# Batch 0's sequence transform folded like the other batches (sums in two equal parts, 60 products become 24), chunk 6 transposed by the DMA crossbar, and fewer, larger crossbar transposes for q and k

## The chip, the core and the metric

One NeuronCore of a Trainium2 chip runs the whole program. The metric is device time in microseconds (us) of one execution. The kernel before takes 269.62 us, the median of 5 runs (268.65 to 270.01). TensorE is called PE, VectorE DVE, ScalarE ACT, GpSimd POOL and SyncE SP, as the profile does. fp16 is used for all matrix operands.

## The reference

```
scores = scale * q @ k^T + bias            # 4 batches, 8 heads, 768 tokens, 64 per head
keep   = 8 global keys, or 0 <= rel < 96   # everything else is masked
x      = softmax(scores) @ v               # heads side by side: 4 x 768 x 512
mixed  = real(fft(fft(x, axis=1), axis=2))
u      = x + mixed
un     = (u - mean(u)) / sqrt(var(u) + 1e-6)
out    = u + relu(un @ w_ch1) @ w_ch2      # 512 -> 2048 -> 512
```

## The kernel before

**Stages of a batch.** Four batches run one after the other, overlapped as far as engines allow. A head pair `hp` (four of them in a batch) is the unit of attention, numbered n = 4b + hp.

1. `load` brings q, k and v of a head pair as fp32; `cast_qk` (batches 0 and 1) and `cast_direct` (batches 2 and 3) turn q and k into fp16.
2. `trans` turns q and k so that the head dimension lies on partitions. Batches 0 and 1 do it on PE with an evacuation (L527, L533, L537). Batches 2 and 3 use `trans_dma` (L506): four crossbar transposes of 64 partitions x 768 from the SP queue for each head pair, one for each half a of the partitions and each token parity t.
3. `score` (L564) makes three groups of banded scores for a head pair, ACT takes the exponential (L584, L587), DVE multiplies with the mask where batches are 2 or 3 (L599), `glob` (L643) adds the scores of the eight global keys, `av` (L691) multiplies with v, and DVE normalises (L710, L711) into X[b].
4. `bounce` writes X[b] to DRAM (L730) and reads it back in another row order as `xr` (L738).
5. The two FFTs are sums on DVE followed by products on PE. Batches 1 to 3 call `fold_s` (L755 to L774: sums that split the sequence of six blocks into residues of 6) and then `fold_d` (L849 to L866: the same along the model dimension, by residues of 4). Batch 0 calls `fold_3` instead (L808, L809, L820 to L830): it only adds and subtracts the two halves of the sequence, in parts of 256, 128 and 128 columns, so that `y_unit` (L892) needs three or six products for each of its 14 outputs, 60 in all, against 24 for another batch. These products use an extra table, `t1x` (480 KB, loaded at L1290 into a buffer of the ring `hT`).
6. `mirror` (POOL, L927 to L940) and `u_unit` (L972, L991 or L1000) end the second FFT, add `xr` and give u and un of a chunk. A batch has three chunks of 256 rows, c = 3b + pr. `nt_unit` turns un: chunks 0 to 6 on PE (L1063, eight matmuls and one evacuation at L1071 or L1073), chunks 7 to 11 by two crossbar transposes of 128 x 512 from SP (`nt_dma`, L1048).
7. `ph_unit` (L1091) multiplies with w_ch1, ACT or DVE evacuates with the relu (L1097, L1098), and `pg_unit` (L1114) or, for chunks 8 to 11, `pg_units` (L1195, seven products in place of eight) multiplies with w_ch2. DVE adds into u and SP stores.

**What sets the order.** The class `Plan` keeps a clock for each engine, costs written by hand, and landing times of some transfers (`LAND`), and issues work in the order in which it would start. So each engine has one fixed instruction list, and every engine and every DMA queue issues strictly in that list's order. PE works through four streams: MIX (y, u, turning of un), ATT, PH and PG. A change of a cost in `Plan` moves instructions but computes nothing else.

**Weights.** w_ch1 and w_ch2 come as eight DMAs that cast (POOL queue, L1345, L1350). They take over the buffers into which batch 1's q and k had been loaded, so the first is issued after the last cast of head pair 7. A small transfer (`hold`, L1359) reads the last piece of w_ch2; batch 2's loads wait for it through `("gate",)`.

**Buffers.** Rings of tiles: `qs` has 3 staging buffers for all loads of batches 2 and 3, `qk` 2 (fp16 q and k before turning), `hT` 3 (the hidden layer of a chunk, but also X[1]), `xx` 2 PSUM double banks plus C and D until the first `ph` takes their place.

Of the kernel before, what the change touches and what calls it, by code (L numbers as in the profile page):

```python
# [17 lines left out]
class Plan:  # L18
# [8 lines left out]
    LAND = {("xw", 0, 0): 36.0, ("xw", 0, 1): 37.6, ("xr", 0): 43.3, ("ld", 4, 2): 50.1, ("ld", 5, 2): 55.5, ("ld", 6, 2): 60.9,  # L27
            ("ld", 7, 2): 66.4, ("w1", 0): 45.8, ("w1", 1): 50.6, ("w1", 2): 54.3, ("w1", 3): 57.9, ("w2", 0): 61.6, ("w2", 1): 65.2, ("w2", 2): 68.1, ("w2", 3): 70.7}
    LAT = {"ACT": 0.14, "DVE": 0.12, "POOL": 0.08}

    def __init__(self):
        self.t = {"PE": 0.0, "ACT": 0.0, "DVE": 0.0, "POOL": 0.0, "SP": 0.7, "DMA": 1.9, "DMA2": 0.0}
        self.tok = {}
        self.ready = []
        self.pending = []
        self.rings = {}
        self.left = {}
        self.n = 0

# [23 lines left out]
    def later(self, ways, needs=(), after=0.0, outs=(), uses=(), ring=None, lat=0.0, dma=0.0, then=None, rank=1):  # L63

        self.n += 1
        self.pending.append((self.n, ways, list(needs), after, outs, uses, ring, lat, dma, then, rank))
        self.promote()
# [11 lines left out]
    def first(self):  # L79

        best = None
        for i, (ready, p) in enumerate(self.ready):
            c = (min(max(self.t[w[0]], r) for w, r in zip(p[1], ready)), p[10], ready[0], p[0], i)
            if best is None or c < best:
                best = c
        return best

    def emit(self, place):
        ready, (_, ways, needs, after, outs, uses, ring, lat, dma, then, _) = self.ready.pop(place)
# [5 lines left out]
        if dma:  # L95
            q = "DMA2" if eng == "ACT" or outs and outs[0][0] in ("xw", "xr") else "DMA"
# [5 lines left out]
        for u in uses:  # L102
            self.used(u, end + lat)
        if ring is not None:
            self.rings[ring].append(end + lat)
# [4 lines left out]
    def pe(self, us, after=0.0):  # L110
# [6 lines left out]
    LOOK = 10  # L117

# [60 lines left out]
def kernel(  # L179
# [24 lines left out]
    DB = 1  # L204
# [78 lines left out]
    NBUF = {"hT": 3, "qk": 2, "qs": 3, "qkT": 4, "er": 2, "eg": 1, "x": 1, "xr": 1, "zy": 1, "eA": 1,  # L283
# [43 lines left out]
    def load(b, hp, which):  # L327
# [3 lines left out]
        if b >= FB:  # L331
            srcs = [(0, q), (1, k)] if which == "qk" else [(2, v)]
            for w, src in srcs:
# [10 lines left out]
                pl.later([("SP", 0.55 if w < 2 else 1.1, run)], free("qs", i) + gate, 0.0, [("ld", n, w)], lat=1.7, dma=2.67)  # L344
# [55 lines left out]
    def cast_direct(b, hp, w, i):  # L400
        n = HP * b + hp

        def cast(on):
            if n not in qk16:
                qk16[n] = buf("qk", n, [P, 2, 2, NP, 2, Dh], FP16, 1)
            for t in range(2):
                copy_on(on, qk16[n][:, t, w], stage[("t", n, w)].rearrange("p (h i t) d -> p t i h d", h=2, t=2)[:, t])
        pl.later([("ACT", act(768), lambda: cast("ACT")), ("POOL", 1.6, lambda: cast("POOL"))],
# [7 lines left out]
    def cast_v0(b, hp):  # L416
        n = HP * b + hp

        def cast():
            V0[n] = buf("er", n, [P, NP, 2, 2, Dh], FP16, 1)  # L420
            nc.gpsimd.tensor_copy(V0[n].rearrange("p n t h d -> p (n t) h d"),
                                  stage[("t", n, 2)].rearrange("p (h n) (t d) -> p h (n t) d", h=2, t=2).rearrange("p h j d -> p j h d"))
        pl.later([("POOL", 0.87, cast)], [("ld", n, 2)] + free("er", n), 0.0, [("vc", n)], [("free",) + vat(n)], rank=b)

    def v_place(b, hp):
        n = HP * b + hp

        def run(start, ring):
# [14 lines left out]
            pl.used(("free", "er", n), e)  # L443
# [43 lines left out]

    def kg_copies(b, hp):
        n = HP * b + hp
        for s in range(2):  # L490
            def cp(s=s):
# [3 lines left out]
                    TT[n][64 * s:64 * s + 64, 1, 0:P].rearrange("p (t m) -> p t m", t=2)[:, :, 0:NG // 2])  # L495
# [3 lines left out]
    def trans_dma(b, hp):  # L499
        n = HP * b + hp  # L500

        def xb(a, t):
            if n not in TT:
                TT[n] = buf("qkT", n, [P, 2, S], FP16, 6)
            o = TT[n].rearrange("p w (i a t m) -> p a t (w i) m", a=2, t=2, m=64)[:, a, t]
            nc.sync.dma_start_transpose(o, qk16[n][64 * a:64 * a + 64, t].rearrange("p w i h d -> p (w i h d)"))  # L506
        at = [(a, t) for a in range(2) for t in range(2)]
        for x, (a, t) in enumerate(at):
            pl.later([("SP", 1.3, lambda a=a, t=t: xb(a, t))],
                     ([("qk", n, 0), ("qk", n, 1)] + free("qkT", n)) if x == 0 else [("xb", n, x - 1)], 0.0,  # L510
                     [("xb", n, x)], lat=0.0, dma=0.01)
        pl.later([("SP", 0.0, lambda: None)], [("xb", n, 3)], 0.0, [("qkT", n)], [("free", "qk", n)], lat=2.2, dma=0.5)
# [28 lines left out]

    def score(b, hp, g):
        n = HP * b + hp
        idx = 2 * HP + 3 * (n - 2 * HP) + g

        def run(start, ring):
            pa = bank(ring, f"sc_{n}_{g}")
            w0, w1_ = ((256, CO), (CO, CO), (256, P))[g]
            tiles = ((2 * g, 0, w0), (2 * g + 1, 256, w1_))
            if b < 2:  # L550
# [10 lines left out]
            for i, c0, cw in tiles:  # L561
                for s in range(2):
                    lo = 64 * s
                    nc.tensor.matmul(pa[:, s, c0:c0 + cw], TT[n][lo:lo + 64, 1, i * P:(i + 1) * P],  # L564
                                     TT[n][lo:lo + 64, 0, i * P:i * P + cw], start=(b > 1), stop=True,
                                     skip_group_check=(b < 2))
            e = pl.pe(0.24 if b > 1 else 0.66, start)
# [17 lines left out]
            if b < 2:  # L585
# [17 lines left out]
        ATT.append(([("qkT", n)] + ([("sid", hp), ("c", "dist")] if b < 2 else []), BANKS(b), run))  # L603
# [29 lines left out]
    def glob(b, halves):  # L633
# [4 lines left out]
        def run(start, ring):  # L638
            pg = bank(ring, f"pgl_{b}_{halves[0]}")
            for half in halves:  # L640
                for i in range(2):
                    hp = 2 * half + i
                    nc.tensor.matmul(pg[32 * half:32 * half + 32, 0, :], kG[b % 2][:, hp, :],  # L643
                                     TT[HP * b + hp][:, 0, 256:S], start=(i == 0), stop=(i == 1),
                                     tile_position=(0, 32 * half))
            e = pl.pe(mm_us(512, 2 * len(halves)), start)
# [14 lines left out]
    XT = [("x", 0), ("hT", 4), ("x", 1), ("x", 2)]  # L661
# [3 lines left out]
    def av(b, part, jp):  # L665
# [8 lines left out]
        def run(start, ring):  # L674
# [31 lines left out]
            def norm():  # L706
                if b not in X:
                    X[b] = buf(XT[b][0], XT[b][1], [P, NS, Dm], FP16, 4 if b else 5)
# [11 lines left out]
    def bounce(b):  # L720
# [3 lines left out]
        for n, (c0, c1) in enumerate(parts):  # L724
            def wr(n=n, c0=c0, c1=c1):
# [3 lines left out]
                for t in range(2):  # L729
# [3 lines left out]
                     lat=1.7, dma=2.4 if b else 2.6)  # L733
# [5 lines left out]
        pl.later([(on, 0.5, rd)], [("xw", b, n) for n in range(len(parts))] + free("xr", b), 0.0, [("xr", b)], lat=1.7, dma=3.8 if b else 2.4, then=None if b else (lambda t: pl.tok.__setitem__(("xi",), pl.t["SP"])))  # L739

    def fold_s(b):

        parts = ((0, 256), (256, 128), (384, 128)) if b == 0 else ((0, 512),)
        c = float(-np.sqrt(3.0) / 2.0)
        for n, (c0, cw) in enumerate(parts):
# [25 lines left out]
            def f4(c0=c0, cw=cw, cell=cell):  # L771
# [7 lines left out]
                     [("f1", b, n)], [("free",) + XT[b]] * (2 if len(hps) == HP else 1))  # L779
            pl.later([("DVE", 2 * dve2(2 * cw), f2)], [("f1", b, n)] + free("ww", IW(b, n)), 0.0, [("f2", b, n)])  # L780
            pl.later([("DVE", 4 * dve2(cw), f3)], [("f2", b, n)], 0.0, [("f3", b, n)])
            pl.later([("DVE", 2 * dve(cw), f4)], [("f3", b, n)], 0.0, [("z", b, n)],
                     [("free", "eA", IA(b, n)), ("free", "ww", IW(b, n))])
        return [("z", b, n) for n in range(len(parts))]

    def IA(b, n):

        return n if b < DB else 2 * b - DB + n

    def NA(b):  # L790
        return 0 if b < DB else 1

    def IW(b, n):

        return 2 * b + n if b < DB else 3 * b - DB + n
# [45 lines left out]
    def fold_d(b, needs):  # L841
# [30 lines left out]
        pl.later([("DVE", 0.95 + 1.0, g1)], needs + free("eA", ia) + free("ww", IW(b, NA(b))), 0.0, [("w", b, 0)])  # L872
        pl.later([("DVE", 0.95 + 1.15, g2)], [("w", b, 0)], 0.0, [("w", b, 1)], [("free", "zy", 2 * b)])
# [169 lines left out]
    def nt_dma(c):  # L1043
        for a in range(2):
            def xb(a=a):
                if a == 0:
                    UNT[c] = buf("unT", c, [P, ND, CH], FP16, 1)
                nc.sync.dma_start_transpose(UNT[c][:, :, a * P:(a + 1) * P], T[("un", c)][:, a])  # L1048
            pl.later([("SP", 1.3, xb)], [("un", c, a)] + (free("unT", c) if a == 0 else [("nx", c, 0)]), 0.0, [("nx", c, a)], lat=0.0, dma=0.01)
# [426 lines left out]
```

## Time and profile before

| | |
|---|---|
| median of 5 runs | 269.62 us |
| the profiled execution | 269.62 us, of which span 267.8 us, clock 0.999 |
| PE busy | 255.3 us, 95% |
| DVE busy | 172.0 us, 64% |
| ACT busy | 151.1 us, 56% |
| POOL busy | 61.4 us, 23% |
| DMA | 42.03 MB, mean 157 GB/s; software queue (weights) 9.3%, SP's queue 50.4% of 16 engines' span |
| crossbar transposes of q and k | 32, landing 3.6 us after issue (median) |
| crossbar transposes of un | 10, landing 2.4 us after issue (median) |
| weights | 8 DMAs of 512 KB, landing 19.0 us after issue (median) |

The profile is of one execution. The span is from its first to its last instruction; 1.8 us of the execution's time lie around it. A busy time counts every moment in which at least one instruction of the engine is under way. Matmuls are pipelined, so the time one takes up in a dense stretch is the distance between starts, not its own duration: 16 matmuls of 256 columns take 1.75 us in the chain of work, 0.109 us each, though each lasts 0.273 us. SPq and ACTq are the queues from which DMAs are issued; the time there is that of the issuing instruction.

### The profile page before, as it was taken

What the parts mean: (1) busy time and instruction counts of PE and PEld (TensorE: products, weight loads), DVE (VectorE), ACT (ScalarE), POOL (GpSimd) and SP (SyncE); (2) the same over time, 40 slices, a digit from 0 to 9 for tenths busy, and PEclk for the clock granted to TensorE, in tenths of its full rate; (3) what the DMA queues carried; (4) which work ended last, traced back from release to release, by engine and by line L of the source; (5) the groups of instructions that cost most, each with busy time, mean ns of one, the idle gap of its engine ahead of it and who ended that gap; (6) DMA issues with size and microseconds to landing.
All of it is one profiled execution on the core that took longest, in us unless ns stands there. A gap on an engine that the chain in (4) does not pass through costs nothing.

```text
span 267.8 us, 6248 instructions
## 1 busy us (share of the span) xinstructions
PE 255.3 (95%) x2540; PEld 181.4 (68%) x2540; DVE 172.0 (64%) x349; ACT 151.1 (56%) x263; POOL 61.4 (23%) x127
## 2 busy tenths in 40 slices
PE   8799899899999899999999999999999999999994
PEld 3454558477855776676575356759777668888883
DVE  4566863833399475861559967778998645525473
ACT  1479693987536737996591354896443345444300
POOL 1442398153010152322110316101100511010000
PEclk9999999999999999999999999999999999999999
DMA  7999959999579986996859895402072251311122
GB/s 212 290 292 305 326 178 224 216 216 212 137 134 257 274 162 136 225 190 146 217 108 204 191 304 138 99 2 42 0 174 103 59 100 39 81 40 42 39 82 78
DMA packets 75743, 42.03 MB, mean 157 GB/s; under 512 B 32834, under 2 KB 71746, under 8 KB 75714
## 3 DMA queue, kind: packets, MB, share of 16 engines
q1 hardware_dynamic: 68658, 32.71, 50.4%
q0 software_dynamic: 4224, 4.19, 9.3%
q10 hardware_dynamic: 2832, 4.72, 7.1%
q8 instruction: 20, 0.33, 0.5%
q14 instruction: 9, 0.07, 0.1%
HBM read 31.92 MB, written 9.44 MB: 154 GB/s over the span
## 4 chain that ended last, share of the span: by engine, by line
PE 64%; DMA 20%; DVE 5%; SPq 4%; POOL 2%; ACT 2%; issue 1%; ACTq 0%; POOLq 0%; DVEq 0%
PE ph L1091 25%; PE pg L1114 12%; DMA w<-in_moe_w_ch_dram 10%; PE pgD L1195 5%; DMA qs<-in_q_dram 5%; PE py L892 4%; PE pgA L1195 4%; PE sc L564 4%; DMA u<-in_v_dram 3%; PE pu L972 3%; PE pav L691 3%; DMA qs<-in_v_dram 2%; SPq L506 2%; PE sc L559 2%; SPq L372 1%
## 5 line engine op out<-in xcount | busy, mean ns | idle before, releaser
L1091 PE MATMUL ph<-unT,w 128*128 128x256 f16 x768 | 94.1, 273 | 2.7 <-ACT hT L1097 1.6
L1091 PEld LDWEIGHTS <-w 128*128 128x128 f16 x768 | 72.6, 98 | 17.1 <-issue 6.2
L1097 ACT ACTIVATE hT<-ph 128x512 f16<-128x512 f32 x78 | 46.2, 597 | 41.6 <-PE ph L1091 41.5
L1114 PE MATMUL pg<-w,hT 128*128 128x512 f16 x256 | 60.7, 379 | 0.0
L1114 PEld LDWEIGHTS <-hT 128*128 128x128 f16 x256 | 24.1, 98 | 23.4 <-issue 0.6
L587 ACT ACTIVATE ex<-sc 128x992 f16<-128x992 f32 (+2 forms) x24 | 20.9, 926 | 8.8 <-PE sc L564 8.8
L584 ACT ACTIVATE er<-sc 128x992 f16<-128x992 f32 (+2 forms) x24 | 21.7, 925 | 5.6 <-PE sc L564 5.1
L376 ACT ACTIVATE qk<-qs 128x384 f16<-128x384 f32 (+1 forms) x29 | 13.8, 528 | 13.4 <-DMA qs<-in_q_dram 5.1
L1098 DVE TENSOR_SCALAR hT<-ph 128x512 f16<-128x512 f32 x18 | 12.4, 691 | 11.2 <-PE ph L1091 11.2
L1123 DVE SCALAR_TENSOR_TENSOR u<-pg,sm,u 128x512 f32<-128x512 f32 x16 | 12.0, 748 | 11.2 <-PE pg L1114 11.2
L466 POOL CAST v<-qs 128x768 f16<-128x768 f32 x8 | 7.0, 880 | 51.7 <-DMA qs<-in_v_dram 51.7
L564 PE MATMUL sc<-qkT 64*128 64x256 f16 (+1 forms) x192 | 17.0, 262 | 0.9 <-ACT er L584 0.8
L599 DVE TENSOR_TENSOR ex<-er,mk 128x992 f16<-128x992 f16 (+2 forms) x24 | 15.1, 636 | 3.8 <-ACT er L584 3.7
L691 PE MATMUL pav<-v,ex 128*128 128x65 f16 x352 | 16.3, 193 | 1.0 <-DVE x L711 0.7
L691 PEld LDWEIGHTS <-ex 128*128 128x128 f16 x352 | 15.2, 97 | 2.4 <-DVE x L711 0.9
L564 PEld LDWEIGHTS <-qkT 64*128 64x128 f16 x192 | 5.9, 94 | 15.1 <-issue 13.3
L1038 POOL TENSOR_SCALAR sm<-sm 128x2 f32<-128x2 f32 x12 | 2.4, 202 | 58.1 <-ACT un L1031 58.0
L907 ACT ACTIVATE zy<-py 128x1024 f16<-128x1024 f32 (+1 forms) x12 | 10.1, 846 | 9.1 <-PE py L892 6.6
L940 POOL COPY ww<-zy 128x512 f16<-128x512 f16 x16 | 9.9, 651 | 22.7 <-PE py L892 20.5
L1031 ACT ACTIVATE un<-un 128x512 f16<-128x512 f16 x24 | 14.9, 626 | 0.1
L991 DVE SCALAR_TENSOR_TENSOR u<-pu,xr 128x512 f32<-128x512 f32 x18 | 11.7, 690 | 4.8 <-PE pu L972 3.2
L1195 PEld LDWEIGHTS <-hT 128*128 128x128 f16 x128 | 12.5, 98 | 1.6
(129 smaller groups left out, 381.9 us busy)
## 6 DMA issues: line engine op xcount, KB each, us to landing
out_dram<-u SPq DMA_DIRECT2D x24, 256.0 KB, 2.4
w<-in_moe_w_ch_dram POOLq DMA_DIRECT2D x8, 512.0 KB, 19.0
qs<-in_q_dram SPq DMA_DIRECT2D x9, 384.0 KB, 5.7
qs<-in_k_dram SPq DMA_DIRECT2D x9, 384.0 KB, 5.3
qs<-in_v_dram SPq DMA_DIRECT2D x16, 192.0 KB, 4.2
xr<-xd ACTq DMA_DIRECT2D x3, 768.0 KB, 5.5
u<-in_v_dram SPq DMA_DIRECT2D x5, 384.0 KB, 6.9
w<-in_q_dram SPq DMA_DIRECT2D x4, 384.0 KB, 6.6
```

What stands on the lines that cost most here:

```text
L376: A(d, s, AF.Copy)
L564: nc.tensor.matmul(pa[:, s, c0:c0 + cw], TT[n][lo:lo + 64, 1, i * P:(i + 1) * P], TT[n][lo:lo + 64, 0, i * P:i * P + cw], start=(b > 1), s ...
L584: A(mine(), cut(pa), AF.Exp, 0.0, 0.125)
L587: A(cut(expst[hp][:, :, g * 512:g * 512 + (384 if g == 2 else 512)]), cut(pa), AF.Exp, 0.0, 0.125)
L599: VT(o, mine(), m, op=ALU.mult)
L691: nc.tensor.matmul(po[:, jj, hh * 65:(hh + 1) * 65], lhsT, v16[b % 2][:, i, h, 0:65], start=(jp == 0 and a == 0), stop=(a == len(ops) - 1) ...
L1031: A(x, x, AF.Square, accum_out=MV[c][:, a, 2:3])
L1091: nc.tensor.matmul(ph[:, a * CH:(a + 1) * CH], W1[0][:, d, jb * P:(jb + 1) * P], UNT[c][:, d, :], start=(d == 0), stop=(d == ND - 1))
L1097: pl.later([("ACT", act(512), lambda: A(dst, ph, AF.Relu)), ("DVE", dve(512), lambda: V.tensor_scalar_max(dst, ph, 0.0))], [], e, [("h", c ...
L1098: ("DVE", dve(512), lambda: V.tensor_scalar_max(dst, ph, 0.0))],
L1114: nc.tensor.matmul(pg, HT[c][:, jb, t * P:(t + 1) * P], W2[0][:, jb, :], start=(jb == 0), stop=(jb == NJ - 1))
L1195: nc.tensor.matmul(o, lhs(j), rhs(j), start=(first and j == 0), stop=(j == NK - 1), skip_group_check=True)
```

## The change

- Batch 0 uses `fold_s` and `fold_d` like the others (`DB` is 0). Its sums run in two parts of 256 columns. `fold_3` and `y_unit`'s branch for it are no longer used, `t1x` isn't loaded, and the buffer indices of `hT`, `eA` and `ww` shift by one. These sums get rank -1 in the planner (`RF`), with a head start of 0.8 us (`AHEAD`).
- Chunk 6 is turned by the crossbar too, and a chunk's un takes one transpose of 128 x 1024 instead of two of 128 x 512. `unT` is laid out (a, d, m) instead of (d, a, m), and `ph_unit`'s moving operand has two runs of 128.
- q of batches 2 and 3 takes one crossbar transpose of 128 partitions x 768, k two of 64 partitions x 768, so three for a head pair instead of four. The cast of q or k becomes one instruction of 768 columns instead of two of 384. q's tokens then lie in another order, so `score` and `glob` read them with strides of 64 elements; a score tile that had 240 columns takes 256, and a `glob` product of 512 columns becomes two of 256.
- v of batches 0 and 1 gets a ring of its own (`v0`) instead of a share of `er`.
- The planner's figures change: landing times, packet times of DMAs, a model of eight DMA lanes, a cost of 0.1 us where PE changes to or from 64-row products. The instruction lists move with them.

The core of the diff (the planner's bookkeeping and index shifts are left out):

```diff
-    DB = 1
+    DB = 0
...
-    LAND = {("xw", 0, 0): 36.0, ("xw", 0, 1): 37.6, ("xr", 0): 43.3, ("ld", 4, 2): 50.1, ...
+    LAND = {("xw", 0, 0): 34.0, ("xw", 0, 1): 36.0, ("xr", 0): 41.0, ("ld", 4, 2): 47.7, ...
...
+            if p[11]:
+                ready = [max(r, self.lanes[p[11] - 1]) for r in ready]
+            c = (min(max(self.t[w[0]], r) for w, r in zip(p[1], ready)) - self.AHEAD * (p[10] < 0), p[10], ready[0], p[0], i)
...
-            for t in range(2):
-                copy_on(on, qk16[n][:, t, w], stage[("t", n, w)].rearrange("p (h i t) d -> p t i h d", h=2, t=2)[:, t])
+            copy_on(on, qk16[n][:, w].rearrange("p n t h d -> p (n t) h d"),
+                    stage[("t", n, w)].rearrange("p (h j) d -> p j h d", h=2))
...
+    def key_at(n, i):
+        return i * P if n < FB * HP else (i % 2) * 384 + (i // 2) * P
+
+    def tile_of(n, lo, w, i, nb=1):
+        x = TT[n][lo:lo + 64, w]
+        if n < FB * HP or w:
+            o = key_at(n, i)
+            return x[:, o:o + P].rearrange("p (t m) -> p t m", t=2)
+        if nb == 1:
+            return x.rearrange("p (i t a m) -> p i a t m", t=2, a=2, m=64)[:, i // 2, i % 2]
+        if i % 2 == 0:
+            return x.rearrange("p (i t a m) -> p i a t m", t=2, a=2, m=64)[:, i // 2]
+        o = (i // 2) * 256 + 64
+        return x[:, o:o + 384].rearrange("p (y q m) -> p y q m", y=2, m=64)[:, :, 0:3:2]
...
-            o = TT[n].rearrange("p w (i a t m) -> p a t (w i) m", a=2, t=2, m=64)[:, a, t]
-            nc.sync.dma_start_transpose(o, qk16[n][64 * a:64 * a + 64, t].rearrange("p w i h d -> p (w i h d)"))
+            if w == 0:
+                nc.sync.dma_start_transpose(TT[n][:, 0].rearrange("p (j x) -> p j x", x=P),
+                                            qk16[n][:, 0].rearrange("p n t h d -> p (n t h d)"))
+            else:
+                nc.sync.dma_start_transpose(TT[n][:, 1, 384 * a:384 * a + 384].rearrange("p (j x) -> p j x", x=64),
+                                            qk16[n][64 * a:64 * a + 64, 1].rearrange("p n t h d -> p (n t h d)"))
...
+                    if b >= FB:
+                        nb = 1 if cw == P else 2
+                        o = pa[:, s, c0:c0 + nb * P]
+                        o = o.rearrange("p (y t m) -> p y t m", y=2, t=2) if nb == 2 else o.rearrange("p (t m) -> p t m", t=2)
+                        nc.tensor.matmul(o, TT[n][lo:lo + 64, 1, key_at(n, i):key_at(n, i) + P], tile_of(n, lo, 0, i, nb), start=True, stop=True)
+                        continue
...
-        parts = ((0, 256), (256, 128), (384, 128)) if b == 0 else ((0, 512),)
+        parts = ((0, 256), (256, 256)) if b == 0 else ((0, 512),)
...
-        for a in range(2):
-            def xb(a=a):
-                if a == 0:
-                    UNT[c] = buf("unT", c, [P, ND, CH], FP16, 1)
-                nc.sync.dma_start_transpose(UNT[c][:, :, a * P:(a + 1) * P], T[("un", c)][:, a])
+        def xb():
+            UNT[c] = buf("unT", c, [P, 2, ND, P], FP16, 1)
+            nc.sync.dma_start_transpose(UNT[c].rearrange("p a d m -> p (a d) m"), T[("un", c)].rearrange("p a f -> p (a f)"))
...
-        if c >= 7:
+        if c >= 6:
             return nt_dma(c)
...
-        def t1x_load():
-            T1X[0] = buf("hT", 3, [P, 5, 384], FP16, 4 * DB)
-            nc.sync.dma_start(T1X[0].rearrange("p a b -> p (a b)"), t1x_d.ap())
```

## The prediction

> **What bounds the kernel now.** I read the busy shares first.
>
> ```profile
> PE 255.3 (95%) x2540; PEld 181.4 (68%) x2540; DVE 172.0 (64%) x349; ACT 151.1 (56%) x263; POOL 61.4 (23%) x127
> ```
>
> PE is the bound, but 95% doesn't say where the other time lies. So next the timeline of PE, for idle time with a releaser (start, duration, row, idle before).
>
> ```profile
> 53.94 2.91 PE L1091 MATMUL ph<-unT,w 128*128 128x256 f16 x24 [1.06 <-ACT ex L587]
> ...
> 88.18 1.03 PE L1091 MATMUL ph<-unT,w 128*128 128x256 f16 x8 [1.65 <-ACT hT L1097]
> ```
>
> These are the two largest stalls after the first microseconds. Setting matmul counts times distances between starts (0.109 us for 256 columns, 0.216 for 512, 0.056 for 128) against the clock, I find about 6 us lost from 5.8 to 37.5 us, none in the y products (37.46 to 44.02), 1.4 from there to 53.94, 1.9 from 82.9 to 89, about 1 in all from 104 to 170, and none from 170 to 253. From 170 on PE is solid: whatever is gained by then, or taken out of PE's work, reaches the end.
>
> Third, the chain of work, for what else holds the start of the middle.
>
> ```profile
> 37.53 3.54 PE py L892 x32
> ...
> 42.50 27.51 DMA w<-in_moe_w_ch_dram
> ```
>
> The weights land until 70.0 us and gate batch 2's loads (70.43). A PE that is ahead meets them.
>
> Fourth, DVE and SP, for the prices of what is added and removed (start, duration; the spacing of starts is what an instruction costs in a row).
>
> ```profile
> 35.39 1.58 DVE L829 TENSOR_TENSOR eA<-zy 128x1536 f16<-128x1536 f16 x1
> ...
> 80.33 0.68 DVE L761 TENSOR_TENSOR ww<-eA 128x1024 f16<-128x1024 f16 x1
> 80.92 0.68 DVE L762 TENSOR_TENSOR ww<-eA 128x1024 f16<-128x1024 f16 x1
> 81.53 0.41 DVE L766 TENSOR_TENSOR zy<-eA,ww 128x512 f16<-128x512 f16 x1
> 81.86 0.42 DVE L767 TENSOR_TENSOR zy<-eA,ww 128x512 f16<-128x512 f16 x1
> 82.20 0.28 DVE L768 TENSOR_SCALAR zy<-ww 128x512 f16<-128x512 f16 x1
> ...
> 83.26 0.68 DVE L773 SCALAR_TENSOR_TENSOR zy<-ww,eA 128x512 f16<-128x512 f16 x1
> ...
> 87.97 0.29 DVE L863 TENSOR_TENSOR ww<-eA 128x256 f16<-128x256 f16 x1
> ```
>
> ```profile
> 96.50 5.21 SPq L506 DMA_TRANSPOSE qkT<-qk  x4
> ...
> 169.24 1.20 SPq L1048 DMA_TRANSPOSE unT<-un  x1
> ...
> 212.10 2.50 SPq L1048 DMA_TRANSPOSE unT<-un  x2
> ```
>
> A crossbar transpose holds SP's queue for 1.2 to 1.3 us, whether it has 64 or 128 partitions.
>
> **What the Trainium skill says.** "TensorE: Matmul & The Clock Gate", section "Wait — 56ns, not 53.3ns?", gives a warm matmul N columns at 2.4 GHz plus about 2.5 ns: 109 ns for 256. The trace agrees (60 y products in 6.56 us). "VectorE: DVE Perf Modes", section on the TRN2 errata, says that an instruction pays a fixed latency, so many small ones pay it often. The trace agrees: 256 columns cost 0.20 us of spacing where 512 cost 0.335, so halving saves less than half. "DMA: Bandwidth & Descriptors", "Rules for kernel authors", advises one transfer of 128 partitions over two of disjoint halves. The rows above show this for SP's queue, not for transfer time, which no row before isolates.
>
> **PE's work.** Counted from the instruction lists of both programs. Batch 0's y: 60 products become 24, 36 x 0.109 = -3.93 us. Chunk 6: eight transposes leave, 8 x 0.056 = -0.45. Scores: 48 tiles of batches 2 and 3 get 16 columns more; the two heads of a pair run at once, so 24 x 16 / 2400 = +0.16. `glob`: 8 products of 512 become 16 of 256, +0.02. Strided reads of q and unT, taken at nothing: the turned q is already written, and the mask broadcast already read, in pieces at full rate; if a matmul of q cost 20% more, 0.3 x 24 groups x 0.2 = +1.4. Sum -4.2.
>
> **DVE's batch 0.** Old sums: 0.94 for the first part (24.31 to 25.25), 1.1 for the two others, then 3.9 (33.46 to 37.4). New, for each part of 256 columns: two of 768 (0.95), two of 512 (0.67), two of 256 (0.41), two scalings (0.3, half-size of a row of 0.20 spacing, bounds 0.2 to 0.4) and two combined ones (0.67; bounds 0.6 to 0.8): 3.0. Then 1.95, and 1.8 as at 86.99 to 88.8; it could be 2.4, since L829's 1.58 shows that this step slows when POOL works. Total 9.8 against 5.9. Where is it paid? The first part comes at 23.85 and pushes the normalisations behind it; DVE has 1.3 us of gaps there, and one evacuation of turned q and k goes to ACT, so x ends at about 32.0 instead of 31.5. Second part to 35.1, first group of sums 37.0, second 39 to 39.6. PE has the same scores and one more turning ahead of y, and gets there at 37.46 + 0.67 = 38.1. So the first y products don't wait, the later ones up to 1.5 us; four y tiles come in 2.6 us where they took 6.56, and their seven evacuations of 0.6 to 0.7 on ACT and DVE no longer hide: PSUM banks come free at about 40.2 to 41. I put the third unit of u at 47.6, and the first `ph` at 51.2 instead of 53.94, behind u's additions on DVE and the exponential of the global scores on ACT. That is 2.7 us, and one placing of v (0.3) is done already: 3.0 of the 3.93.
>
> **The weights' stage.** From 51.2 PE needs weight pieces. Issued 37 to 43, landing 19.0 us later in the median, the last at 70.0: one every 3.4 us or so. v of head pair 7 queues among them. The table without t1x: 480 KB at about 290 GB/s is 1.65 us that all behind it on SP may win; bound 0 if the weights' issue, after the last cast at 36 us, sets the pace. I take 1.2. The part of PE's list before the second half of batch 1's `av` (70.15 us) then ends at about 68.2 with one `pg` block (0.86) more done: 2.8 us ahead; without the 1.2, 1.6.
>
> **The stall at 88.** It came from the masks on ACT (1.35 us) ahead of an evacuation, after PE had run through ten `pg` blocks. In the new lists all masks come together behind the bounce, and PE has twelve `pg` blocks (10.4 us, to about 84.4) in front of chunk 2; y's sums are ready at about 85. So 1.65 comes back: 4.45 us ahead at 104.
>
> **Batches 2 and 3.** SP loses 8 transposes of q and k and 4 of un: 12 x 1.25 = 15 us of its queue (9 if a 128-row one costs 1.5 times). Before, head pair 10's casts waited until 102.9 for a `qk` buffer, freed by the last of these. Casts: 14 pairs of 0.94 us on ACT become 10 of 0.845, -4.7; POOL does 6 instead of 2, at 0.83, with v's casts, the mirror and the rstd behind them. PE stalls little there, so I book 0, from -1 to +1.
>
> **Chunk 6.** A wait is added: SP waits for un, then 1.2 to 2.5 us of issue and 2.4 us landing, in place of 0.45 + 1.02. Queued behind it on SP are k's last transposes and chunk 7. Cover, from the end of its u: in the old run 6.5 us passed until its `ph` (163.9 to 170.41), filled with `pg`, u and scores, and the new list has the same. Un is ready about 2.8 in, so 6.4 to 7.7 are needed: +0 to 1.2; I take 0.2.
>
> **Sum.** Ahead at 104 us by 4.45; chunk 6's PE work -0.45 and its wait +0.2; scores and `glob` +0.18; batches 2 and 3 otherwise 0: -4.52. The profiled execution took 269.62 us (span 267.8 and 1.8 around it), which is also the median: 269.62 - 4.52 = 265.1 us.
>
> **Rivals.**
> 1. *The weights take it back.* For it: 27.5 us of chain are their transfer, and PE arrives sooner. Against: chunks 0 and 1 hold 14 us of `ph` that need only w_ch1. If t1x frees nothing and two `pg` blocks wait for w_ch2, 1.6 us remain at 70 and the stall at 88 is half kept: -2.2, 267.4.
> 2. *The stalls vanish too.* Shorter SP and ACT queues and the end of both named stalls: -4.2 - 1.06 - 1.65 = -6.9, 262.7. Against it: evacuations of y are bunched.
> 3. *Slower, by chunk 6 on the crossbar.* If its transpose stands in SP's list behind head pair 15's load and transposes: 5.7 landing, 0.9 cast, three issues 3.9, its own 1.2 + 2.4 = 14.1 us against 6.5 of cover, 7.6 lost, 4.2 won: 273.0. It decides from a wait of 4.4 us. Against: these transposes were issued before 169 us in the old run, un of chunk 7 did not wait for them, and there are fewer.
> That the change doesn't do what it says is excluded by the instruction lists.
>
> **Chances.** Forecast (263.8 to 266.6) 0.45; rival 1 (to 268.6) 0.22; rival 2 0.20; rival 3 0.07; within 0.3%, about what a measurement of this kernel can tell from no change, 0.06. So faster 0.87, same 0.06, slower 0.07. Range 261.8 to 268.6: it leaves out the slower case, most of no change and the far end of rival 2.
>
> **What would show it.** Right: 24 y products in under 4.5 us; first `ph` near 51; no stall of over 1 us near 85; PE solid from about 166. Wrong: `ph` at 54 (DVE's sums cost more), idle PE between 56 and 68 with a DMA as releaser (rival 1), chunk 6's first `ph` waiting for unT (rival 3), or distances of more than 0.109 us in `ph`.

## The result, and the profile after

The changed kernel takes 271.72 us (median of 43 runs, 267.34 to 275.81), the kernel before 269.71 (median of 80 runs, 268.42 to 272.69). The ratio is 0.9991 with a 95% interval of 0.9972 to 1.001. It counts only runs within 1.5% of a kernel's fastest, which leaves out more than half of the changed kernel's, so it lies below the quotient of the medians, 1.0075. A gain isn't shown: by the ratio the two are the same, by the medians of all runs the changed kernel is 2.0 us slower, and its own runs spread over 8.5 us. The forecast, 265.1 us and faster with a chance of 0.87, did not come true; its range ended at 268.6.

The profiled execution took 270.91 us, span 268.8. First the busy shares.

```profile
PE 253.2 (94%) x2504; PEld 178.3 (66%) x2504; DVE 179.4 (67%) x367; ACT 146.7 (55%) x243; POOL 64.8 (24%) x129
```

PE has 2.1 us less to do than before and the span is 1.0 longer. So PE's work went and its waits grew. The timeline of PE shows which waits stand in place of the two shown of before:

```profile
40.68 1.03 PE L947 MATMUL py<-t,ww 128*128 128x256 f16 x8 [0.80 <-ACT qkT L571]
...
52.79 1.91 PE L1144 MATMUL ph<-unT,w 128*128 128x256 f16 x16 [1.17 <-DVE u L1055]
...
90.03 1.03 PE L1144 MATMUL ph<-unT,w 128*128 128x256 f16 x8 [1.59 <-ACT hT L1150]
...
101.46 0.27 PE L1027 MATMUL pu<-t,zy 128*128 128x128 f16 x2 [0.99 <-DVE u L1046]
```

The first `ph` comes 1.15 us sooner than before, and the stall at 88 has not gone: it stands at 90 with the same releaser, and others follow. Over 36 to 53 us PE is busy 14.47 of 17.00 where it was busy 16.88: in that stretch the work taken out of it became waiting.

ACT's timeline shows why its evacuation (L1150) comes so late.

```profile
77.61 5.13 ACT L1359 ACTIVATE mk<-dist 128x640 f16<-128x640 f16 x8 [2.50 <-issue]
88.65 0.84 ACT L392 ACTIVATE qk<-qs 128x768 f16<-128x768 f32 x1 [5.92 <-DMA qs<-in_k_dram]
88.73 0.36 ACTq L790 DMA_DIRECT2D xr<-xd  x1
89.40 0.58 ACT L1150 ACTIVATE hT<-ph 128x512 f16<-128x512 f32 x1
```

The masks are done at 82.7, as forecast. But the next instruction in ACT's list is the cast of k of head pair 9, and ACT stands idle for 5.92 us until that k has landed. Behind it wait the read of `xr` and the evacuation. The chain of work says why k came late (start, duration, what).

```profile
70.99 5.08 DMA qs<-in_v_dram
...
76.19 0.84 POOL v L482
...
77.04 5.86 DMA qs<-in_q_dram
...
82.96 1.23 POOL qk L396
...
84.20 0.38 SPq L388
```

Load, cast, load, cast, load, one after the other: q of pair 9 is issued the moment the cast of v of pair 8 ends, and k of pair 9 (84.20) the moment q's cast ends. The releasers in the trace, which are inferred, say that all three use the same one of the three `qs` buffers, and that the other two had been free since about 75 us; pair9_fixed and pair9_spoiled below confirm it. The same in SP's list:

```profile
77.04 0.37 SPq L388 DMA_DIRECT2D qs<-in_q_dram  x1
77.51 4.10 SPq L538 DMA_TRANSPOSE qkT<-qk  x1
84.20 0.38 SPq L388 DMA_DIRECT2D qs<-in_k_dram  x1
```

One transpose holds the queue for 4.10 us here. The prediction's 1.2 to 1.3 us isn't the whole range: in before, too, one at 80.47 held it for 2.71.

Last, DVE's sums for the second part of batch 0:

```profile
34.05 0.91 DVE L821 TENSOR_TENSOR zy<-eA,ww 128x256 f16<-128x256 f16 x1
34.89 0.90 DVE L822 TENSOR_TENSOR zy<-eA,ww 128x256 f16<-128x256 f16 x1
35.72 0.21 DVE L823 TENSOR_SCALAR zy<-ww 128x256 f16<-128x256 f16 x1
```

The first two take three times as long as the same sum in fold_in_turn (0.28, shown below); POOL casts two tiles of q and k at that time (33.92 to 35.66).

### The profile page after: what moved, and what is told of

Its sections match the earlier page's. It is cut to its first block, busy times and chain, and to the rows that moved or that the text cites. A ratio compares the mean times of both kernels' runs of the same rounds, so it can differ in the third digit from the quotient of the medians.

```text
span 268.8 us, 6141 instructions
## 1 busy us (share of the span) xinstructions
PE 253.2 (94%) x2504; PEld 178.3 (66%) x2504; DVE 179.4 (67%) x367; ACT 146.7 (55%) x243; POOL 64.8 (24%) x129
## 4 chain that ended last, share of the span: by engine, by line
PE 52%; DMA 25%; ACT 7%; DVE 6%; POOL 3%; issue 3%; SPq 3%; POOLq 0%; DVEq 0%; ACTq 0%
PE ph L1144 19%; PE pg L1167 13%; DMA w<-in_moe_w_ch_dram 9%; PE pgD L1248 5%; DMA out_dram<-u 5%; PE pgA L1248 4%; DMA qs<-in_v_dram 4%; DMA u<-in_v_dram 3%; DMA qs<-in_k_dram 3%; PE pav L743 2%; ACT er L629 2%; PE py L947 2%; DMA qs<-in_q_dram 2%; SPq L388 2%; PE pu L1027 2%
## 5 line engine op out<-in xcount | busy, mean ns | idle before, releaser
L1150 ACT ACTIVATE hT<-ph 128x512 f16<-128x512 f32 x75 | 44.6, 598 | 47.9 <-PE ph L1144 47.7
L1151 DVE TENSOR_SCALAR hT<-ph 128x512 f16<-128x512 f32 x21 | 14.5, 690 | 13.7 <-PE ph L1144 13.4
L644 DVE TENSOR_TENSOR ex<-er,mk 128x992 f16<-128x992 f16 (+2 forms) x24 | 17.5, 738 | 2.0 <-ACT er L629 1.6
L392 ACT ACTIVATE qk<-qs 128x768 f16<-128x768 f32 x11 | 9.3, 842 | 14.2 <-DMA qs<-in_k_dram 8.0
L763 DVE TENSOR_TENSOR x<-pav,rc 128x512 f16<-128x512 f32 (+1 forms) x21 | 12.9, 615 | 0.7
L1077 ACT ACTIVATE un<-u,sm 128x512 f16<-128x512 f32 x10 | 7.1, 721 | 11.4 <-DVE sm L1050 11.4
L962 ACT ACTIVATE zy<-py 128x1024 f16<-128x1024 f32 (+1 forms) x10 | 8.8, 899 | 7.0 <-PE py L947 6.4
```

The source lines that it names most:

```text
L644: VT(o, mine(), m, op=ALU.mult)
L763: VT(X[b][:, 2 * jp:2 * jp + 2, first * Dh:(first + nh) * Dh].rearrange("p j (h d) -> p j h d", d=Dh), pv[:, :, :, 0:Dh], rc.to_broadcast( ...
L1150: pl.later([("ACT", act(512), lambda: A(dst, ph, AF.Relu)), ("DVE", dve(512), lambda: V.tensor_scalar_max(dst, ph, 0.0))], [], e, [("h", c ...
L1151: ("DVE", dve(512), lambda: V.tensor_scalar_max(dst, ph, 0.0))],
```

## Experiments

"Before" and "after" are the two kernels. Times are medians in us, then their range, then the ratio to before with its 95% interval. Differences between kernels are differences of medians.

### The parts alone

**fold_alone**: before with only batch 0's sums folded.

```diff
-    DB = 1
+    DB = 0
...
-        parts = ((0, 256), (256, 128), (384, 128)) if b == 0 else ((0, 512),)
+        parts = ((0, 256), (256, 256)) if b == 0 else ((0, 512),)
...
```

> The kernel before with one part of the change: batch 0's sums in two parts of 256 columns as for the other batches, 24 products of y, no t1x table; transposes, chunk 6 and the planner's figures as before. Theory A (the 3.9 us of PE work are gained at first, and given back later by loads and transposes of batches 2 and 3): some 1 to 2.5 us faster than before, 267 to 268.6, and the first ph 1 to 3 us earlier than 53.94. Theory B (the longer sums on VectorE and the bunched evacuations eat the saving on the spot): within 0.5 us of 269.7, the first ph at 53 to 54.

Measured: 272.86 (270.88 to 274.48), 1.0105 [1.0067, 1.0142]: slower. First `ph` at 53.44, only 0.5 sooner, and one stall of 3.32 us at 110 (`ph` behind ACT's evacuation). The fold alone does not pay. Whether a stall this large, 57 us later, is the fold's own doing isn't settled by this run; fold_in_turn below tests it.

**undo_chunk6**: after with chunk 6 turned on PE again.

```diff
-        if c >= 6:
+        if c >= 7:
```

> The changed kernel with chunk 6 turned on PE again (eight matmuls and an evacuation), all else as changed. If the wait for the crossbar costs at chunk 6 what its PE work saved (0.45 us), the time stays within 0.5 us of the changed kernel; if it is what takes the gain back (stalls of 1.6 us between 160 and 180 us), it is 1.5 us or more faster.

Measured: 272.57 (268.28 to 275.34), 1.0027 [1.0, 1.0054]: 0.9 above after's median, with the same wide spread. Chunk 6 by the crossbar is not the loss.

**undo_qk**: after with the four transposes, the halved casts and the score tiles of 240 columns of before, under the new planner. The lines show one of its places.

```diff
...
-        for x, (w, a) in enumerate(((0, 0), (1, 0), (1, 1))):
+        for x, (a, t) in enumerate(at):
...
```

> The changed kernel with q and k of batches 2 and 3 turned as before: four crossbar transposes of 64 partitions for a head pair, casts in two halves, score tiles of 240 columns. Theory C (the crossbar transpose of 128 partitions is the slow part, it lands 5.1 us after issue in the median where one of 64 partitions took 3.6): 2 to 3 us faster than the changed kernel, about 267, and a narrower spread of times. Theory A: no gain, 270 to 272, since SP gets eight transposes more.

Measured: 286.66 (283.38 to 289.35), 1.055 [1.051, 1.059]. Much slower, by a list that falls apart in batch 3 (PE waits of up to 3.75 us between 160 and 182, and a granted clock down to about half there). This tells of a bad list, not of what a transpose costs.

### The staging buffers

The ring `qs` doesn't give its buffers out in turn: which one a load gets follows from the order in which the plan issues loads and casts. **slots_in_turn** is after with load i in buffer i mod 3; the lists of all engines stay as they are.

```diff
+        if tag == "qs":
+            return wk.tile(shape, dtype, tag=f"qs{i % 3}_", name=f"{tag}_{i}", bufs=1)
         return wk.tile(shape, dtype, tag=tag, name=f"{tag}_{i}", bufs=NBUF[tag])
```

> The changed kernel with the three staging buffers of batches 2 and 3 handed out strictly in turn; instruction lists and their order are the same. In the changed kernel k of head pair 9 is given the buffer that q of the same pair has just left (its load is issued at 84.20, when q's cast ends), while two buffers have been free since 75 us. Theory A: k of pair 9 is issued at about 81 or earlier, its cast on ScalarE no longer holds up the evacuation behind it, the stall at 90.03 (1.59 us) and the wait for xr until 100 shrink: 1.5 to 3 us faster than the changed kernel, 268 to 270. Theories B and C: within 0.5 us of it.

Measured: 267.1 (266.49 to 267.23), 0.9889 [0.9867, 0.991]: 4.6 below after in the medians (span 265.2 against 268.8), and faster than before. After's quickest runs (267.34) come close to it, and by the two ratios the gap is 2.7. Its SP and ACT, beside the same rows of after above:

```profile
74.04 0.37 SPq L390 DMA_DIRECT2D qs<-in_q_dram  x1
...
76.03 0.50 SPq L390 DMA_DIRECT2D qs<-in_k_dram  x1
```

```profile
84.88 0.35 ACTq L792 DMA_DIRECT2D xr<-xd  x1
84.98 0.72 ACT L1361 ACTIVATE mk<-dist 128x640 f16<-128x640 f16 x1
85.61 0.83 ACT L394 ACTIVATE qk<-qs 128x768 f16<-128x768 f32 x1
87.78 0.60 ACT L1152 ACTIVATE hT<-ph 128x512 f16<-128x512 f32 x1 [1.34 <-PE ph L1146]
```

K's load goes out 8.2 us sooner. ACT now waits for PE, not PE for ACT, and PE has no stall of 0.3 us or more from 80 to 158 us. Batch 3's first y product starts at 152.19; in after it starts at 155.80, 3.6 later, as the spans say.

**pair9_fixed** and **pair9_spoiled** test that it is this one pair. A string of letters names the buffer of each load: fixed (first line) keeps after's own choice and puts only pair 9 in turn; spoiled (second line) is in turn and puts q and k of pair 9 on v8's buffer, after which k of pair 10 takes the one of v of pair 9 and the turn goes on from there.

```diff
+        if tag == "qs":
+            return wk.tile(shape, dtype, tag=f"qs{'ACBACBACBACABCABCACCCABCABBAB'[i]}_", name=f"{tag}_{i}", bufs=1)
...
+        if tag == "qs":
+            return wk.tile(shape, dtype, tag=f"qs{'ABCABCABBBCACBACBACBACBACBACB'[i]}_", name=f"{tag}_{i}", bufs=1)
```

> The changed kernel with its own assignment of staging buffers, but for head pair 9: q, k and v of this pair take the three buffers in turn (in the changed kernel q takes the one that v of pair 8 leaves, and k the one that q leaves). Theory A1 (this one assignment is the cause of what slots_in_turn won back): 267 to 268, spread under 2 us. Theory A2 (all of the assignments of batches 2 and 3 together do it): 269 to 271.

> Buffers in turn everywhere, but for head pair 9, where q takes the one that v of pair 8 leaves, and k the one that q leaves. Theory A1: it puts back most of the loss, 269.5 to 272, with a stall of over 1 us before the third ph of chunk 2 near 90 us. Theory A2: 267 to 268.5.

Measured: fixed 267.23 (266.04 to 267.76), 0.9903 [0.9876, 0.9931]; spoiled 272.4 (271.81 to 273.96), 1.0108 [1.0077, 1.014]. One pair's buffers take the whole difference away and bring it back. In fixed, k and v of pair 12 and q of pair 13 still follow one another on one buffer and cost nothing that can be measured: sharing a buffer isn't a loss in itself, and here it was one where an evacuation that PE needs stands behind the load. The stall in the spoiled one:

```profile
92.39 1.46 PE L1146 MATMUL ph<-unT,w 128*128 128x256 f16 x8 [3.27 <-ACT hT L1152]
93.65 1.91 PE L949 MATMUL py<-t,ww 128*128 128x256 f16 x8
```

**before_in_turn** and **fold_in_turn** give the same buffers to before and to fold_alone.

> The kernel before with its three staging buffers handed out in turn; instruction lists as before. Of the kernel before, q of head pair 9 takes the buffer that v of pair 8 has just left. Theory A (the order in which buffers are handed out hid what the change is worth): it gains little, 0 to 1.5 us, so 268 to 269.7, since its stall at 88 us came from the masks and not from a load; the change is then worth what lies between this and the 267.1 of the changed kernel in turn. Rival: the whole 2.6 us come from the buffers and the change is worth nothing; then it is at 267 too.

> The kernel before with batch 0's new sums alone, and staging buffers in turn. fold_alone lost 3.7 us in one stall at 109.97, before ph, which ScalarE released late. Theory A: that stall goes with the buffers, and the time falls from 272.9 to 267 to 269. Theory B (the new sums cost on VectorE what they save on PE): it stays at 270 or above.

Measured: 268.86 (267.62 to 271.68), 0.9977 [0.9961, 0.9994], and 269.56 (269.1 to 271.38), 1.0005 [0.9986, 1.0023]. Before gains 0.9 from it, fold_alone 3.3: its stall at 110 was of this kind too. With the buffers out of the way the fold is worth +0.7 (slower) on top of before by the medians; the two intervals overlap, so it is no gain rather than a loss.

### The parts with the buffers in turn

**undo_c6_in_turn** and **undo_qk_in_turn** repeat the two undoings on slots_in_turn.

> The changed kernel with chunk 6 on PE again and staging buffers in turn. If the crossbar for chunk 6 hides as forecast (0.45 of PE saved, 0.2 of wait added) it is 0.2 to 0.5 us slower than 267.1; if its wait costs more than it saves (PE stalls 1.3 us between 160 and 180 in the changed kernel in turn), it is faster, 266 to 267.

> The changed kernel with q and k turned in four crossbar transposes again and staging buffers in turn. undo_qk took 286.7. Theory A: most of that was the buffers too, and it comes to 267 to 271; the distance to 267.1 is what the larger transposes and casts are worth. Rival: four transposes do not fit the planner's new figures in any case, and it stays above 275.

Measured: 267.61 (266.49 to 269.28), 0.9927 [0.9909, 0.9946], so chunk 6 is worth 0.5 by the medians, with intervals that just overlap; and 285.4 (282.51 to 286.91), 1.056 [1.0515, 1.0605]. The bad list of undo_qk isn't the buffers' doing: in it PE waits 3.75 us for DVE ahead of batch 3's y. It says nothing of the transposes' worth, so they were taken another way: **old_figures_in_turn** is after's computation in the order that before's planner figures give, and **no_fold** is that without the fold (`DB`, `fold_3` and `t1x` come back). Two of the places of old_figures_in_turn:

```diff
...
-                ready = [max(r, self.lanes[p[11] - 1]) for r in ready]
-            c = (min(max(self.t[w[0]], r) for w, r in zip(p[1], ready)) - self.AHEAD * (p[10] < 0), p[10], ready[0], p[0], i)
+            c = (min(max(self.t[w[0]], r) for w, r in zip(p[1], ready)), p[10], ready[0], p[0], i)
...
```

> The changed kernel's computation ordered with the planner's figures and rules of before (landing times, packet times, no lanes, no head start for batch 0's sums), buffers in turn. If the new figures do nothing but move instructions about, it is within 1 us of 267.1. If the gain over before_in_turn (1.8 us) is theirs, it is at 268.9 or above, as fold_in_turn was (269.6, old figures too).

> The changed kernel without its first part: batch 0's sums, 60 products and t1x table as before; larger transposes and casts of q and k, chunk 6 on the crossbar, v0 ring, the planner's figures of before, buffers in turn. Its pair is old_figures_in_turn (266.8), the same with the new sums. Theory E (the new sums gain little, since VectorE's longer chain holds the start of y; the gain over before_in_turn, 268.9, is that of the transposes, casts and chunk 6): 266.5 to 267.8. Rival (the sums gain their 3.9 us of PE work only where SP and ScalarE are relieved, which fold_in_turn did not have): 268.9 to 270.5.

Measured: 266.79 (265.9 to 268.38), 0.9903 [0.9869, 0.9938], and 267.77 (266.84 to 269.28), 0.9928 [0.9896, 0.9959]. So the new figures bring nothing (266.8 with the old, 267.1 with the new). The fold brings 1.0 with overlapping intervals. The larger transposes and casts with chunk 6 and v's ring bring 1.1 without the fold (268.86 to 267.77) and 2.8 with it (269.56 to 266.79).

### Where the fold's 3.93 us went

The second half of batch 1's `av` starts between 69.97 and 70.53 in before, before_in_turn, slots_in_turn, no_fold and old_figures_in_turn, and at 69.08 in after, where v of batch 1 was cast earlier. Such places differ by about 1 us from profile to profile. But a start of 2.8 us sooner, as forecast, is in none of them, although the fold lets one more `pg` block pass before it in slots_in_turn. Where PE lost the time depends on the lists.

In before's order (old_figures_in_turn against no_fold, and fold_in_turn against before_in_turn) the loss comes ahead of y. Up to 36 us PE is busy 29.67 with the fold and 32.30 without it, so PE has 2.6 us more of waiting there; from 36 to 70 the two are alike (32.99 and 32.74). The other pair shows the same (30.03 and 32.29). That leaves 1.3 of the 3.93, and 1.0 is what the times say. In old_figures_in_turn PE waits for DVE three times, where no_fold's waits in that stretch are 0.74, 0.36 and 0.52:

```profile
28.67 0.22 PE L719 MATMUL pav<-vG,eg 128*128 128x130 f16 x1 [1.19 <-DVE x L750]
...
31.44 1.51 PE L548 MATMUL pt<-ident,qk 128*128 128x128 f16 x24 [1.11 <-DVE x L750]
...
34.57 0.39 PE L596 MATMUL sc<-qkT 64*128 64x256 f16 x4 [1.20 <-DVE qkT L554]
```

DVE is then at the longer sums of batch 0's first part, ahead of two of the normalisations (L750) that PE waits for. The first of these end at 28.52 and 29.74, in no_fold at 26.90 and 28.00.

With the new figures and the head start of 0.8 us (slots_in_turn) PE loses nothing there: 32.20 up to 36 us. It loses it after: 30.22 from 36 to 70, 2.5 less than no_fold. These waits are for ACT's evacuation of turned q and k (0.80, ahead of y), for DVE's additions of u (1.17, ahead of the first `ph`), and for v of batch 1:

```profile
50.16 0.36 PE L455 MATMUL pvp<-v,ident 64*64 64x128 f16 x12 [0.36 <-POOL v L439]
...
61.44 0.36 PE L455 MATMUL pvp<-v,ident 64*64 64x128 f16 x12 [1.01 <-POOL v L439]
```

**weights_first** puts batch 0's mirror on POOL behind the issue of all eight weight DMAs; all weights are then issued sooner.

```diff
-                     [("y", b) + y for y in ys] + free("ww", IW(b, NA(b) + 1)) + [("rv", b, n - 1)][:n], 0.0,
+                     [("y", b) + y for y in ys] + free("ww", IW(b, NA(b) + 1)) + [("rv", b, n - 1)][:n] + [("wl", 7)] * (b == 0), 0.0,
```

> The changed kernel with buffers in turn, and the mirror copies of batch 0 on GpSimd placed behind all eight weight DMAs, not between them. In slots_in_turn GpSimd idles 1.8 us before the first copy (42.60), then issues the last two weight DMAs (0.75 each) between copies, and rev is ready at 46.05, 1.5 us later than it need be. Theory D (this order holds u, and so the first ph at 52.82): first ph 0.7 to 1.5 us earlier, time 266 to 266.5. Rival (VectorE's chain from the sums to the sixth addition sets it anyway): within 0.3 us of 267.1.

Measured: 268.87 (267.27 to 270.75), 0.997 [0.9948, 0.9991], 1.8 slower than slots_in_turn. The mirror is ready at 44.5 instead of 46.05 and the last u of batch 0 is added a microsecond sooner, yet the first `ph` comes at 54.41, since v of head pair 4 lands later. PE waits 2.26 us for it, and over the next 4 us its granted clock was 0.57, which is part of the 1.8. POOL's cast of it in slots_in_turn and in weights_first:

```profile
49.29 0.82 POOL L439 CAST v<-qs 128x768 f16<-128x768 f32 x1 [1.81 <-DMA qs<-in_v_dram]
```

```profile
51.17 0.83 POOL L439 CAST v<-qs 128x768 f16<-128x768 f32 x1 [4.47 <-DMA qs<-in_v_dram]
```

**sums_short** and **stt_first** change DVE's sums of batch 0's second part: sums_short leaves out half of four residues (so its output is not the whole computation), stt_first takes them in another order.

```diff
...
+                if b == 0 and c0:
+                    return
...
```

> slots_in_turn, with four of the eight kinds of instruction in the second part of batch 0's sums left out (two additions, two scalings of 256 columns; half of four residues of batch 0 are zero, so its output is not the whole computation). They take 1.9 us there, 33.85 to 35.78, of which 1.2 by GpSimd's casts running at the same time. Theory E: y's second group starts 1.2 to 1.9 us earlier than 40.47, the first ph 0.7 to 1.5 us earlier than 52.82, time 265.6 to 266.5. Rival (the first ph is held by what follows y: mirror, additions of u): within 0.4 us of 267.1.

> slots_in_turn, with the second part of batch 0's sums in another order: the two instructions that multiply and add first, then the scalings, the plain additions last, so that GpSimd's casts (33.72 to 35.45) run beside the former. In slots_in_turn an addition of 256 columns took 0.90 beside a cast, and 0.28 in fold_in_turn without one. If only plain additions are slowed, the sums end 0.8 to 1.2 us earlier (y's second group at 39.3 to 39.7), time 266 to 266.8. If the others are slowed alike, nothing changes: 267.1 within 0.3.

Measured: 266.71 (265.21 to 269.6), 0.9874 [0.9827, 0.9922], and 265.92 (265.81 to 267.75), 0.9863 [0.9822, 0.9904]; both intervals overlap that of slots_in_turn. With fewer sums DVE's part took 7.6 us where it took 8.3 in slots_in_turn, so only 0.7 less, and y's second group began no sooner (40.75; 40.47 in slots_in_turn): ACT's evacuation of turned q and k, which it also needs, ended at 40.70. Later PE waited 1.92 us for v and 0.79 for ACT, the first `ph` came at 53.62, later than with all the sums, and 16 `ph` products took 3.26 us instead of 1.91, at a granted clock of 0.50 over 54 to 56. So in these lists 0.7 us less on DVE brings nothing, since ACT's evacuation ends at the same time; that DVE's chain never sets the end isn't shown. The other order only moved the slow instructions, while POOL cast from 35.66 to 37.53:

```profile
35.80 1.04 DVE L841 SCALAR_TENSOR_TENSOR zy<-ww,eA 128x256 f16<-128x256 f16 x1
36.77 0.84 DVE L825 TENSOR_SCALAR zy<-ww 128x256 f16<-128x256 f16 x1
37.53 0.21 DVE L826 TENSOR_SCALAR zy<-ww 128x256 f16<-128x256 f16 x1
```

**table_once** and **table_thrice** add a load of 480 KB that nobody uses, once or three times, on SP ahead of batch 1's v.

```diff
+            if b == 1:
+                for x in range(3):
+                    pl.later([("SP", 0.0, lambda: nc.sync.dma_start(mk[:, 0:3, :].rearrange("p a b -> p (a b)"), t1x_d.ap()))], [("xi",)])
```

> slots_in_turn with one transfer more that nothing uses: the 480 KB table that the change removed is loaded again, on SP ahead of batch 1's v, into the masks' buffer. All instruction lists but SP's are the same. Theory F (until 70 us the DMA engines are the bound, so PE's early lead meets the weights and v, and only the bytes saved count): the last weight, and so batch 2's first load, comes 1 to 1.7 us later than 68.87, and the time is 0.6 to 1.5 us above 267.1. Rival (PE and VectorE set the pace there, the transfer is hidden): within 0.3 us of 267.1.

> The same with the transfer three times (1440 KB). Theory F: batch 2's first load 3.5 to 5 us later than 68.87, time 3 to 5 us above 267.1. Rival: under 1 us above.

Measured: 268.56 (267.16 to 269.69), 0.9947 [0.9923, 0.997], and 281.31 (279.75 to 282.26), 1.0417 [1.0381, 1.0452]: +1.5 and +14 on slots_in_turn. Once, batch 2's first load went out at 71.14 instead of 68.87; but the first weight DMA was 1.0 late in that profile before the table went out, so about 1.3 can be the table's. PE's wait for v also cost clock: 16 `ph` products took 3.28 us instead of 1.91, nearly as much as the whole +1.5. Thrice, it didn't move further (about 69), where 3.5 to 5 us later was expected. Instead SP waited 14.0 us: the three loads write one buffer, and each waited for the one before to land, with v behind them in the list:

```profile
64.26 0.54 PE L455 MATMUL pvp<-v,ident 64*64 64x128 f16 x12 [14.36 <-POOL v L439]
```

So what stands on SP right ahead of v costs time at the end. What the bytes alone cost isn't shown by table_thrice, and table_once puts the table right ahead of v, where before had it 9 us ahead. The pair that has the table in its old place is no_fold, which loads it, and old_figures_in_turn, which doesn't: there batch 2's first load goes out at 69.17 and 68.90.

## Why the prediction was wrong

**The step that failed most: "Casts: 14 pairs of 0.94 us on ACT become 10 of 0.845 ... PE stalls little there, so I book 0, from -1 to +1."** I counted SP's and ACT's instructions and read that POOL takes six casts, but not which buffer each load waits for. In the new order q and k of pair 9 fall behind v of pair 8 on one buffer, and that chain of load and cast ends in ACT's list ahead of an evacuation that PE needs. It cost 3.6 us in the profiled spans and 4.6 in the medians. That this pair's buffers are the cause is shown both ways, by pair9_fixed and pair9_spoiled.

**"The stall at 88 ... 1.65 comes back."** Half right: the masks did move, and PE did have its twelve `pg` blocks. Another instruction took their place ahead of the evacuation. With the buffers in turn the step held, and the smaller stalls from 104 to 160 went too, part of rival 2.

**"I put the third unit of u at 47.6, and the first `ph` at 51.2."** Third u 48.51, first `ph` 52.79. Batch 0's second sums were mis-sized: 0.41 for two of 256 columns, measured 1.67 (34.05 to 35.72). The Trainium skill has the reason in "SBUF — State Buffer", "Who interferes with whom": a DVE instruction with two operands in SBUF and a POOL instruction that reads SBUF exclude each other for a whole instruction. The trace agrees: in fold_in_turn, whose POOL casts nothing then, the same sum takes 0.28.

```profile
35.18 0.28 DVE L768 TENSOR_TENSOR zy<-eA,ww 128x256 f16<-128x256 f16 x1
```

I had noted that this step slows when POOL works, and had not looked where the new list puts POOL's casts. But without this mis-sizing y's second group would hardly have started sooner in these lists: it also needs ACT's evacuation of turned q and k, which ended as late as DVE's sums (40.41 and 40.38 in slots_in_turn), and sums_short shows no gain.

**"Then ends at about 68.2 with one `pg` block more done: 2.8 us ahead."** In after's profile `av` starts at 69.08 with that block done, 1.9 ahead; in slots_in_turn 0.7. In the times the fold is worth between -1.0 and +0.7. The failed step is that 3.0 of the 3.93 would be won by the first `ph`, with the longer sums paid mostly in DVE's gaps. In the old order they didn't fit into those gaps, and PE lost 2.3 to 2.6 us ahead of 36 us. In the new order PE lost 2.5 us more than no_fold between 36 and 70 us, in waits for v (1.4 us), for DVE (1.2) and for ACT (1.0), where no_fold waits 1.3 in all: rival 1 came true in part. The table's 1.2 is not shown: in the one pair that has it in its old place batch 2's first load moves by 0.3.

**Chunk 6: -0.45 + 0.2.** Measured -0.5 (267.61 to 267.1), with intervals that just overlap; consistent with it. Its first `ph` has no wait for unT. Rival 3 did not come.

**Reads with strides at nothing.** Right for `ph`: 16 products in 1.75 us, 0.109 each. The scores' columns were not isolated.

**"PE solid from about 166."** Failed: from 160 to 180 it loses 1.2 us in after and as much in slots_in_turn, behind ACT's exponentials of batch 3's scores. In old_figures_in_turn there is no such stall, and its span is 1.0 less than that of slots_in_turn (264.2).

**The sum.** Predicted 265.1. Take the buffers from after and 267.1 remains; the other 2.0 are about what the fold did not bring (2.8 forecast at 70, 0.7 found in slots_in_turn's profile), with stalls that went elsewhere and some that stayed at 160 to 180.

**Open.** How the 1.1 to 2.8 divide among transposes, casts and v's ring was not separated, since with four transposes the new planner gives a list that is bad for other reasons. After's times spread over 8.5 us in 43 runs; in turn they spread over 0.7 in only 5 runs, in pair9_fixed over 1.7 in 6, in undo_c6_in_turn over 2.8 in 22. That fits a chain that sometimes closes in time and sometimes doesn't; no profile of a quick execution of after shows it.

The six quickest complete kernels here are stt_first, old_figures_in_turn, slots_in_turn, pair9_fixed, undo_c6_in_turn and no_fold (265.9 to 267.8); all are faster than before and after. One of them, no_fold, is without the fold, which was the largest term of the forecast.

## What to carry to other kernels

When a change moves loads or casts in an in-order list, follow each buffer: which load waits for which cast, and what is queued on that engine behind the next cast. A ring of three buffers isn't three buffers' worth of cover unless they are given out in turn. And work taken out of PE is worth what the next landing transfer lets through: look first at what PE will wait for at the earlier time, here DVE's normalisations in one order, and ACT, DVE and v in the other.

## What the runs showed of the hardware

After a stall of 3.27 us PE also lost its clock. The stretches of 4 us from 88 on in pair9_spoiled (length, busy time and count of PE, PEld, DVE, ACT and POOL, then granted clock, DMA share, GB/s):

```profile
88.00:92.00 4.00, 1.12 (x11) 0.86 (x9) 2.22 (x7) 0.98 (x2) 0.00 (x0) 1.00 1.12 235
92.00:96.00 4.00, 3.60 (x19) 2.56 (x19) 0.00 (x0) 2.25 (x4) 0.83 (x1) 0.61 1.12 331
96.00:100.00 4.00, 4.00 (x53) 3.73 (x52) 2.71 (x6) 1.82 (x3) 3.08 (x7) 0.97 1.15 322
```

At 0.61 of the clock the 3.60 us in which PE was busy do the work of 2.2, so by an estimate from these figures the stall costs about 1.4 us more than its length; eight y products took 1.91 instead of 1.04. The stall of 3.32 in fold_alone was followed by 0.65. After's stall of 1.59 and before's of 1.65 were followed by 1.00. In weights_first a stall of 2.26, which ends at 52.05, was enough:

```profile
52.00:56.00 4.00, 3.95 (x35) 2.44 (x35) 1.53 (x3) 2.91 (x7) 0.95 (x2) 0.57 1.20 216
```

The Trainium skill, "TensorE: Matmul & The Clock Gate", "What's actually happening", gives a window of about 3.4 us without work after which the clock is halved. The runs here show the drop after less: undo_qk's stall of 2.15 us was followed by 0.57 over 90 to 94, and in table_once two of 1.71 and 0.79, with little work between them, by 0.57 over 54 to 58.

A POOL cast beside DVE slows more than one kind of instruction: sums of 256 columns from 0.28 to 0.91, combined ones from 0.41 to 1.04, scalings from 0.21 to 0.84, each by 0.63. And a crossbar transpose of q, 128 partitions by 768, lands later than one of 64 partitions: in after those of q landed 5.1 us after issue in the median (2.7 to 12.6), those of k 3.5 (2.4 to 10.6), where the 64-partition ones of before took 3.6.
